# Attention scores of two batches with the keys in chunks of 128, 128, 128 and 64, where two pairs of heads share the chunk of 64

## The chip, the core and the metric

The kernel runs on one core of one Trainium2 chip. The metric is the device time of one execution in microseconds (us), lower is better. A core has engines that run at the same time, each through its own list of instructions in order: TensorE (PE, with its weight loads shown as PEld), VectorE (DVE), ScalarE (ACT), GpSimd (POOL) and SyncE (SP). Transfers between the main memory and the core's memory (SBUF) are issued from SP, ACT or POOL and run on 16 DMA engines. Products land in PSUM, a small memory that PE writes and that DVE and ACT read.

## What is computed

Attention with a softmax that has one added to its sum, and then a feed-forward layer with a squared ReLU:

```python
scores = scale * np.matmul(q, k.transpose(0, 1, 3, 2))
m = np.max(scores, axis=-1, keepdims=True)
e = np.exp(scores - m)
attn = e / (np.sum(e, axis=-1, keepdims=True) + np.exp(-m) + 1e-09)
x = np.matmul(attn, v)        # then laid out as 3584 tokens x 768
...
h = x @ w_in
r = np.maximum(h, 0.0)
out = (r * r) @ w_out
```

There are 8 batches, 12 heads, 448 positions and 64 numbers per head; w_in is 768 x 2048 and w_out 2048 x 768. All inputs are fp32; the kernel computes in fp16 with fp32 sums. It takes the exponentials without subtracting the maximum, so that the sum becomes sum(exp) + 1.

## The kernel before

**Layout.** Two heads make a pair (6 pairs in a batch): the queries and keys of a pair lie transposed in the tile `qk`, one head on rows 0 to 63 and the other on rows 64 to 127. A batch has 448 keys. They are taken in RUN = 4 chunks of P = 112; token 4p + s is row p of chunk s, since each partition loads four consecutive tokens. For a chunk, `scores` (L178) makes keys x queries in PSUM (tile `sp`, 112 rows, both heads side by side), one `exp` (L168) turns that into fp16 in the tile `et`, `add_chunks` (L209) adds the four chunks on DVE, `row_sums` (L239) sums over the 112 rows by a product with `ones` and makes the reciprocal of 1 + sum on ACT with a logarithm and an exponential (tile `rcp`), `values` (L232) makes the products of the four chunks with `vn` (tile `xp`), and `normalise` (L257) multiplies the two into `xt`, the input of the feed-forward layer.

**Units.** A unit is one pair and a range of its queries. Batch 0 is cut into queries 0 to 191 (units 0 to 5) and 192 to 447 (units 6 to 11), so that the feed-forward layer of its first 192 tokens can begin early. Batch 1 has units 12 to 17, batch 2 units 18 to 23, and so on. In the half units of batch 0 one exp takes two chunks (112 x 768 or 112 x 1024 numbers); in the others one exp takes one chunk of both heads (112 x 896).

**Start.** Batch 0's first three pairs are loaded as fp32 by SP (queries) and ACT (keys) into two buffers of the pool `e` (`load_natural`, L83), which has four buffers in all and also gives the `et` tiles: units 0 and 1 get the other two, and unit 2 gets the one that held the queries once they have been read. `cast` (L144) makes them fp16, 16 small transposes per pair on PE put both operands into one PSUM bank `tp` (`transposes`, L153), and DVE copies `tp` to `qk` (L164): for the first three pairs in two copies of half of the tokens, for the others in one. The other loads, all of `vn` among them (`load_v`, L77), are issued by POOL, which converts to fp16 on the way. Batches 1 and 2 are transposed in the same manner; from batch 3 on the transposes are done by DMA.

**Order.** The order of each engine's list is written out by hand. Loop L494 runs units 0 to 5, L523 units 6 to 11 and L561 units 12 to 17; in each, PE gets scores of the unit, transposes of a later pair, values and row sums of earlier units, and in between `drain` (L430) lets through so many steps of the first feed-forward product (`tile_in`, L297). At the end of unit 17 what is left of these is run (L590), then the row sums of unit 17 (L591). From L623 on, batches 2 to 7 go in groups of three units, with the second product (`tile_out`, L340) between the scores. Waits are set by the framework: an instruction waits for what it reads, and for the last readers of a buffer that it overwrites. PSUM has two buffers for `sp`, one for `xp` and three for `mp` (transposes, row sums, feed-forward).

In `et` of a half unit, chunk and head are addressed like this:

```python
return et[:, 0:RUN * 2 * n].rearrange("p (c h j n) -> p c h j n", c=2, h=2, j=2)[:, c, :, kk % 2, :]
```

The softmax here doesn't subtract the row's maximum and nothing guards it: scores larger than these inputs give would overflow.

## Time and profile before

The median of three runs is 412.54 us (412.3 to 412.69). The profiled execution took 412.49 us, of which 410.6 lie between its first and its last instruction (the span).

| | busy us | share of the span |
|---|---|---|
| PE | 401.0 | 98% |
| PEld | 259.0 | 63% |
| DVE | 289.8 | 71% |
| ACT | 234.4 | 57% |
| POOL | 36.3 | 9% |

"Busy" is the union of an engine's instructions; matmuls overlap and their ends are modelled, so a busy PE is not yet one at its peak. TensorE's clock was granted in full throughout (0.999). Some dates: the first exp starts at 6.78 us, unit 6's first at about 19 us, unit 12's first at 36.30 us, unit 17's row sums stand at 67.21 us, and the groups of three units begin right after. A group line gives the source line, engine, operation, output and inputs with their shapes, the count, then the total and the mean of one, and last the idle time of the engine ahead of it with what ended it.

### The profile page before, as it was taken

The page shows a single profiled execution, that of the slowest core. Times are in us where ns is not written, and L with a number is a line of the kernel's source. Part 1 is how long each engine was busy: PE and PEld are TensorE (multiplying, and loading weights), DVE is VectorE, ACT ScalarE, POOL GpSimd, SP SyncE. Part 2 cuts the span into 40 slices and gives each one's busy share as a digit, 9 for nine tenths or more (in the row PEclk, how much of TensorE's full clock was granted, in tenths as well). Part 3 has the DMA queues.
Part 4 walks back from the last instruction along what each step waited for, and adds up shares of the span by engine and source line. Part 5 has one row for each costly group of instructions (what it writes and reads, how often), then busy time and mean ns, then how long its engine had stood idle before and what let it go on. Part 6 is the DMA issues. An engine that isn't in the chain of part 4 may idle for free.

```text
span 410.6 us, 10685 instructions
## 1 busy us (share of the span) xinstructions
PE 401.0 (98%) x4715; PEld 259.0 (63%) x4715; DVE 289.8 (71%) x554; ACT 234.4 (57%) x312; POOL 36.3 (9%) x58
## 2 busy tenths in 40 slices
PE   7899998999999999999999999999999999999997
PEld 3577676755576666666566666667566665555664
DVE  3778896978976787777876788867876789186000
ACT  5998997667393745559383755739464663100111
POOL 7524030020000200001000030001000000000000
PEclk9999999999999999999999999999999999999999
DMA  9999999689114891499304992297102010010222
GB/s 203 197 198 197 203 202 219 127 132 219 60 42 107 135 219 25 98 183 182 100 2 114 168 179 64 77 188 124 41 2 69 11 41 2 38 40 0 78 77 78
DMA packets 75823, 45.58 MB, mean 111 GB/s; under 512 B 42560, under 2 KB 72000, under 8 KB 75456
## 3 DMA queue, kind: packets, MB, share of 16 engines
q0 software_dynamic: 28848, 22.16, 35.6%
q1 hardware_dynamic: 46208, 22.05, 23.1%
q8 instruction: 37, 0.61, 0.6%
q10 hardware_dynamic: 720, 0.69, 0.5%
q14 instruction: 10, 0.08, 0.1%
HBM read 45.69 MB, written 17.93 MB: 155 GB/s over the span
## 4 chain that ended last, share of the span: by engine, by line
PE 89%; ACT 4%; DVE 4%; DMA 1%; issue 1%
PE mp L286 24%; PE mp L352 17%; PE mp L288 11%; PE xp L286 8%; PE sp L201 6%; PE xp L352 5%; PE mp L236 5%; PE xp L288 3%; PE xp L236 3%; PE sp L189 3%; ACT et L169 3%; PE mp L250 2%; PE mp L158 1%; DMA et<-in_k_dram 1%; DVE qk L164 1%; ACT rcp L253 1%
## 5 line engine op out<-in xcount | busy, mean ns | idle before, releaser
L169 ACT ACTIVATE et<-sp 112x896 f16<-112x896 f32 (+2 forms) x144 | 125.2, 915 | 40.7 <-PE sp L201 30.6
L352 PE MATMUL mp<-wout,gs 64*128 64x384 f16 x896 | 115.2, 322 | 0.0
L286 PEld LDWEIGHTS <-win 128*64 128x64 f16 x1536 | 83.9, 110 | 45.6 <-issue 1.5
L286 PE MATMUL mp<-xt,win 128*64 128x448 f16 (+2 forms) x1200 | 107.0, 323 | 0.3 <-DVE qk L164 0.2
L293 DVE TENSOR_SCALAR rt<-mp 128x448 f16<-128x448 f32 (+2 forms) x96 | 59.7, 622 | 26.3 <-PE mp L286 13.8
L352 PEld LDWEIGHTS <-gs 64*128 64x128 f16 x1152 | 58.1, 94 | 21.1
L295 DVE TENSOR_TENSOR gs<-rt 128x448 f16<-128x448 f16 (+2 forms) x128 | 50.2, 392 | 4.4
L352 PE MATMUL xp<-wout,gs 64*128 64x384 f16 x256 | 53.1, 323 | 0.0
L253 ACT ACTIVATE rcp<-mp,one_b 128x448 f32<-128x448 f32 (+2 forms) x42 | 26.5, 630 | 41.9 <-PE mp L250 41.7
L361 ACT ACTIVATE ot<-mp 128x384 f32<-128x384 f32 (+1 forms) x16 | 7.6, 477 | 64.5 <-PE mp L288 48.2
L201 PE MATMUL sp<-qk 64*112 64x224 f16 x480 | 43.1, 258 | 0.0
L169 ACT ACTIVATE nn<-sp 112x896 f16<-112x896 f32 x48 | 41.7, 917 | 1.6
L201 PEld LDWEIGHTS <-qk 64*112 64x112 f16 x480 | 30.6, 128 | 14.2 <-issue 3.6
L286 PE MATMUL xp<-xt,win 128*64 128x448 f16 x336 | 36.5, 352 | 0.0
L288 PEld LDWEIGHTS <-gs 128*128 128x128 f16 x256 | 24.4, 98 | 15.1 <-issue 0.4
L236 PEld LDWEIGHTS <-vn 112*64 112x64 f16 x432 | 22.4, 109 | 15.4 <-issue 3.9
L288 PE MATMUL mp<-wout,gs 128*128 128x384 f16 (+1 forms) x192 | 30.3, 317 | 0.0
L214 DVE TENSOR_TENSOR es<-et 112x896 f16<-112x896 f16 x30 | 18.7, 623 | 15.8 <-ACT et L169 15.3
L254 ACT ACTIVATE rcp<-rcp 128x448 f32<-128x448 f32 (+2 forms) x48 | 27.7, 577 | 1.5
L189 PE MATMUL sp<-qk 64*112 64x448 f16 (+2 forms) x192 | 25.8, 320 | 1.4 <-ACT et L169 0.6
L216 DVE TENSOR_TENSOR es<-es,half 112x896 f16<-112x896 f16 x42 | 26.2, 623 | 1.0
L293 DVE TENSOR_SCALAR rt<-xp 128x448 f16<-128x448 f32 x32 | 19.9, 622 | 8.2 <-PE xp L286 6.7
(63 smaller groups left out, 340.0 us busy)
## 6 DMA issues: line engine op xcount, KB each, us to landing
vn<-in_v_dram POOLq DMA_DIRECT2D x7, 672.0 KB, 9.0
out_dram<-ot SPq DMA_DIRECT2D x9, 384.0 KB, 2.3
win<-in_moe_w_in_dram POOLq DMA_DIRECT2D x8, 384.0 KB, 14.2
wout<-in_moe_w_out_dram POOLq DMA_DIRECT2D x4, 768.0 KB, 18.0
stage_q<-in_q_dram POOLq DMA_DIRECT2D x4, 676.0 KB, 11.3
stage_k<-in_k_dram POOLq DMA_DIRECT2D x4, 676.0 KB, 14.7
out_dram<-ot SPq DMA_DIRECT2D x8, 288.0 KB, 9.0
out_dram<-ot SPq DMA_DIRECT2D x9, 192.0 KB, 2.7
```

The lines of the kernel that those rows point to most:

```text
L169: nc.scalar.activation(out=out_, in_=in_, func=AF.Exp, scale=scale)
L189: nc.tensor.matmul(sp[:, h, o:o + n], qk[r, 1, x + P * kk:x + P * kk + P], qk[r, 0, x + q0:x + q0 + n], start=True, stop=True)
L201: nc.tensor.matmul(sp[:, odd, h * (S // 2):(h + 1) * (S // 2)], qk[r, which, kx:kx + 2 * P - 1:2], qk[r, 0, x:x + S // 2], start=True, sto ...
L216: nc.vector.tensor_add(es, es, half[:, 0:2 * S])
L236: nc.tensor.matmul(xp[64 * h:64 * h + 64, o:o + n], vns[b][:, 2 * pr + h, kk, :], of_head(chunk(et, u, kk // 2, kk), u, h), start=(kk == 0 ...
L253: nc.scalar.activation(out=rcp[:, 0:m], in_=zp[:, 0:m], func=AF.Ln, bias=one_b)
L254: nc.scalar.activation(out=rcp[:, 0:m], in_=rcp[:, 0:m], func=AF.Exp, scale=-1.0)
L286: nc.tensor.matmul(out_[x:x + 64], lhsT[:, x:x + 64], rhs, start=start, stop=stop)
L288: nc.tensor.matmul(out_, lhsT, rhs, start=start, stop=stop)
L293: nc.vector.tensor_scalar(out=rt[:, 0:m], in0=hp[:, 0:m], scalar1=0.0, scalar2=None, op0=ALU.max)
L295: nc.vector.tensor_mul(gs[:, f0:f0 + per, t0 % RING:t0 % RING + n], r, r)
L352: nc.tensor.matmul(o[:, 0:w], g[x:x + 64], wout[x:x + 64, fb, n0:n0 + w], start=(fb == 0), stop=(fb == NFFB - 1))
```

## The change

Batches 0 and 1 (`WIDE`) take their keys in three chunks of 128 and one of 64. Key 3p + kk, for keys 0 to 383, is row p of chunk kk; keys 384 to 447 are the last chunk. Two neighbouring pairs share one tile for the last chunk: pair j of the two on rows 64j to 64j + 63, so that one exp serves both. One unit of the two "owns" it: the odd one among units 0 to 5, the even one among units 6 to 17. The owner's `et` is kept until the other unit's values are done.

- **Exps.** The unit that isn't the owner has 3 chunks instead of 4: in batch 1 three exps instead of four, in batch 0 a second exp of half size. All have 128 rows instead of 112.
- **Scores.** The last chunk is four products of 64 x 64 tiles (two heads, two pairs) instead of two of 64 x 112.
- **Sums.** DVE adds only the three chunks of 128 (two additions, from four chunks in three, or in batch 0 two, of which one was double size). `row_sums` has a second product per head, of the shared chunk with `halves`, a matrix that is 1/256 on the unit's own 64 rows and zero on the others.
- **Values.** The last product of a head has 128 rows of `vn`, of which the other pair's 64 are zero; DVE clears them at the start, for both batches (`clear_v`).
- **Loads.** `vn` of these batches comes in 128 partitions of 3 tokens, and the last 64 tokens in four loads more (`load_last_v`): for batch 0 as fp32 from SP and ACT, into the unused end of the two buffers that hold the raw queries and keys, whence DVE converts them in unit 1 (`cast_last_v`); for batch 1 from POOL.
- **Copies to `qk`.** The keys are put into the order of the tokens while they are copied, which reads `tp` with a step of 112 numbers; the queries keep their order. So a pair of these batches has two copies instead of one, the first three pairs of batch 0 three instead of two (keys; queries 0 to 191; queries 192 to 447). Pair 0's first copy of queries is made by ACT.
- **Buffers.** From unit 18 on every third `et` lies in one of the two `nn` buffers, in turn, where it was two in six before, beginning with unit 22. Batches 2 to 7 compute as before.

```diff
     def load_v(b, p0, p1):
...
+        if b in WIDE:
+            nc.gpsimd.dma_start(out=vns[b][:, hs, 0:RW], in_=v[b, hs, 0:SW].rearrange("h (p t) d -> p h t d", t=RW))
...
+    def load_last_v(b):
+        for j in range(2):
+            for h in range(2):
+                to, src = last_v(b, j, h)
+                if b:
+                    nc.gpsimd.dma_start(out=to, in_=src)
+                else:
+                    (nc.sync, nc.scalar)[j].dma_start(out=raw_v(j, h), in_=src)
...
+    def cast_last_v():
+        for j in range(2):
+            for h in range(2):
+                nc.vector.tensor_copy(last_v(0, j, h)[0], raw_v(j, h))
+
+    def clear_v(b):
...
+        for j in range(2):
+            nc.vector.memset(rows[64 - 64 * j:128 - 64 * j, j, :, :, RW, :], 0.0)
...
-        parts = (0, S // 2, S) if b == 0 and pr < 3 else (0, S)
-        for x, y in zip(parts, parts[1:]):
-            nc.vector.tensor_copy(qks[b][:, 0:2, pr * S + x:pr * S + y], tp[:, :, x:y])
+        o = qks[b][:, :, pr * S:(pr + 1) * S]
+        if b not in WIDE:
+            nc.vector.tensor_copy(o[:, 0:2], tp[:, :, 0:S])
+            return
+
+        nc.vector.tensor_copy(o[:, 1].rearrange("p (n s) -> p n s", s=RUN), tp[:, 1, 0:S].rearrange("p (s n) -> p n s", s=RUN))
+        if b == 0 and pr < 3:
+            if pr == 0:
+                nc.scalar.activation(out=o[:, 0, 0:FIRST], in_=tp[:, 0, 0:FIRST], func=AF.Copy)
+            else:
+                nc.vector.tensor_copy(o[:, 0, 0:FIRST], tp[:, 0, 0:FIRST])
+            nc.vector.tensor_copy(o[:, 0, FIRST:S], tp[:, 0, FIRST:S])
+        else:
+            nc.vector.tensor_copy(o[:, 0], tp[:, 0, 0:S])
...
+    def wide_scores(u, et, c, last):
+        b, pr, q0, n = u
+        qk = qks[b]
+        kks = (0, 1) if c == 0 else (2, 3) if last else (2,)
+        two = [] if n == S else s_psum.tile([128, 2, 512], FP32, name="sp")
+        for kk in kks:
+            sp = s_psum.tile([128, 2, 512], FP32, name="sp") if n == S else two
+            o = 0 if n == S else kk % 2 * n
+            pairs = (pr,) if kk < RW else (pr // 2 * 2, pr // 2 * 2 + 1)
+            for h in range(2):
+                r = slice(64 * h, 64 * h + 64)
+                for j, of in enumerate(pairs):
+                    x = of * S
+                    keys = slice(x + kk, x + SW, RW) if kk < RW else slice(x + SW, x + S)
+                    to = slice(0, 128) if kk < RW else slice(64 * j, 64 * j + 64)
+                    nc.tensor.matmul(sp[to, h, o:o + n], qk[r, 1, keys], qk[r, 0, x + q0:x + q0 + n],
+                                     start=True, stop=True)
...
+            if u[0] in WIDE:
+                nc.vector.tensor_add(es, (e[:, 0], es)[step], e[:, 1 + step])
...
+            nc.vector.tensor_add(s, (e[:, 0, :, 0], s)[step], (e[:, 0, :, 1], e[:, 1, :, 0])[step])
...
+            parts = [(ones, total), (halves[:, u[1] % 2], last_chunk(i))] if u[0] in WIDE else [(ones[0:P], total[0:P])]
...
+        if i >= 3 * NPAIR and i % 3 == 2:
+            ets[i] = nat.tile([128, RUN * 2 * S], FP16, name=f"nn{i // 3 % 2}")
...
+    def owns(i):
+
+        return i % 2 == (i < NPAIR) and units[i][0] in WIDE
...
         if i:
             sums(i - 1)
+        if i == 1:
+            cast_last_v()
         if i > 1:
-            scores(u, et, 1)
+            visit(i, 1)
```

## The prediction, made before the change was run

> **What bounds the kernel now.** I read the page's first part, then busy time by stretch, then the chain of work that ended last, and the groups by form for prices.

> ```profile
> PE 401.0 (98%) x4715; PEld 259.0 (63%) x4715; DVE 289.8 (71%) x554; ACT 234.4 (57%) x312; POOL 36.3 (9%) x58
> ```

> PE bounds the whole, but the change lies in the first 69 us (batches 0 and 1). Busy time there, by stretch (start:end, length, busy us and count per engine, clock, DMA share, GB/s):

> ```profile
> 6.00:10.40 4.40, 3.88 (x61) 2.12 (x61) 3.23 (x10) 3.62 (x6) 2.64 (x4) 1.00 1.40 212
> 10.40:18.30 7.90, 7.39 (x123) 4.62 (x122) 6.14 (x14) 7.44 (x12) 4.55 (x6) 1.00 1.46 197
> 18.30:36.30 18.00, 16.33 (x296) 12.34 (x295) 14.10 (x29) 15.76 (x20) 5.46 (x7) 1.00 1.45 197
> ...
> 42.60:67.20 24.60, 23.05 (x356) 16.72 (x355) 22.04 (x42) 20.69 (x28) 3.51 (x5) 1.00 1.38 207
> ```

> The columns after the length are PE, PEld, DVE, ACT, POOL. Units 2 to 5 (second line) are ACT's: 7.44 of 7.90 us. In units 6 to 11 (third) ACT and PE are both nearly full; from unit 13 on (last line) PE has 1.55 us idle in 24.6 and DVE 2.6. The chain says the same step by step:

> ```profile
> 9.52 0.69 DVE qk L164 x2
> ...
> 21.43 1.54 ACT et L169 x2
> ...
> 36.30 3.35 ACT et L169 x4
> ...
> 47.24 0.53 PE sp L189 x4
> 47.76 0.31 PE mp L250 x2
> 48.08 0.76 PE xp L236 x8
> ...
> 66.53 0.64 DVE es L216
> 67.21 0.40 PE mp L250 x2
> ```

> The reader is to see three things: DVE's copies to `qk` carry the start; ACT's exps carry the middle; PE carries batch 1, until one wait of 1.13 us at its end, where PE stands for unit 17's sums. Products of 64-row halves run two at a time (eight of 448 in 0.76 us, 0.19 per two), and a group of another tile shape costs about 0.15 us more (four score products 0.53 instead of 0.38). After 69 us PE is full in every stretch that I looked at, up to 110 us, so a shift of that point goes through to the end.

> Prices, from the groups by form:

> ```profile
> L169 ACT ACTIVATE et<-sp 112x1024 f16<-112x1024 f32 x12 | 11.8, 1016 | 1.0 <-PE sp L189 0.7
> L169 ACT ACTIVATE et<-sp 112x768 f16<-112x768 f32 x12 | 9.4, 806 | 1.0 <-PE sp L189 0.9
> L164 DVE COPY qk<-mp 128x896 f16<-128x896 f16 x14 | 8.4, 618 | 1.0 <-PE mp L158 1.0
> L164 DVE COPY qk<-mp 128x448 f16<-128x448 f16 x6 | 2.1, 386 | 2.2 <-PE mp L158 2.2
> ```

> [...] The new copy of the keys reads with a step of 112[...] contiguous fp16 from PSUM 386 ns for 448 numbers, fp32 from PSUM (L293, 128x448) 622; no row shows a stepped fp16 read. [...] four 64x64 tiles at once are not in the trace.

> **The change, part by part.**

> *Exps (ACT, removed).* Batch 1: three exps of 0.917, 2.75 us. Batch 0: from the two rows above a number costs 0.82 ns, so half sizes take 0.49 and 0.60: three times 0.32 and three times 0.42, 2.2 us. Pair 0's copy of 192 queries adds about 0.33 (L361 takes 277 ns for 128, 383 for 256). 128 rows cost what 112 do, since 896 numbers per row stay 896.

> *DVE.* Sums: batch 1 loses one addition of 0.623 per unit, 3.7 us; batch 0 swaps 0.551 + 0.358 for 2 x 0.358 and 0.689 + 0.422 for 2 x 0.422, 6 x 0.19 + 6 x 0.27 = 2.8. Copies to `qk`: 0.62 (keys, stepped) + 0.386 for 0.618, +0.39 in nine pairs; the first three go from 0.77 to 0.91 (pair 0) and 0.62 + 0.25 + 0.29 = 1.16 (the two rows give 154 ns + 0.518 per number). In all +4.4. If the stepped read cost nothing extra, 0.386, it would be +1.6; I take 0.62. Four casts of 64x192: the one near row is 0.43 for 512 (L150), a memset of 64 takes 0.11; I take 0.25 each, 1.0 in sum, ends 0.5 and 1.7. Zeroing `vn` and `halves`, about 1.3 us, lies in the 3.24 us in which DVE waits for the first queries: nothing, unless POOL's first `vn` load (1.49 us) has to wait for the zeros. That is at most 0.6 for the rest of POOL's queue, the fourth pair's loads among it, which land just ahead of their transposes at 10.27. DVE's total hardly moves; its place does.

> *PE.* Row sums: two products more per unit, 0.19 (448), 0.11 (256), 0.08 (192). Last chunk: per two units two score pairs become one set of four tiles, less one pair's time, but with one more change of shape, 0.15. Net per two units: 2 x 0.19 − 0.19 + 0.15 = 0.34, three times = 1.0 in batch 1; 0.26 and 0.23 in batch 0's halves, three times each = 1.5. If four tiles don't overlap, 0.19 more per two units (+0.6 in batch 1); if the change of shape is hidden, 0.45 less.

> *Start, units 0 to 5 (to 18.25 us, unit 5's second exp).* The keys' copy starts at 5.92 as before. Keys 0.62, ACT's copy 0.33 after it: unit 0's scores at 6.95 (6.36 before). DVE is then 0.6 late for the next cast, and pair 1's scores need 0.62 + 0.25 where one copy of 0.386 was enough: 9.1 (8.13). Pair 2 in the same way: copies done at 11.6. Now a **new wait**: unit 2's exps write the buffer that held the raw queries, and that is free only after `cast_last_v`, which stands on DVE behind those copies and unit 0's sums (0.66 with overlap): three casts later it is 12.9, against 10.38 in the trace: +2.5[...]. Behind the waiting exp on ACT stand all other exps; PE waits with them, since `sp` has two buffers. From there ACT has two half exps less (−0.64), but DVE, with the keys' copies of pairs 3 to 5 (+1.17, less four sums at 0.19), is now last at the row sums: +0.4. I take **+2.0** at unit 5's end; ends +1.0 and +2.9.

> *Units 6 to 11.* ACT loses 1.26, but PE has only about 1.0 us idle between 20.3 and 36.3 and gains 0.7 of work; unit 5's sums are 0.2 shorter. The gain is cut off by PE: **−0.3**, ends −0.9 and +0.4.

> *Units 12 to 17.* Unit 13 has its exp less where PE now waits 0.41 for ACT (42.56): −0.4. At the end one addition instead of two stands behind the last `drain`: −0.6 of the 1.13. PE's work +1.0. Other ACT savings are slack: ACT has 3.9 us idle there. **0.0**, ends −0.9 and +0.8.

> *Loads.* SP and ACT issue two more each (0.46 us a piece), ahead of ACT's table load; ACT idles 1.28 us after it: nothing. They land behind the third pair's, which took 6.0 us at most from issue; the casts come at 12.2: nothing. POOL's four more for batch 1 go behind a load issued at 25.48 that lands 16.4 us later, at 41.9; first use is 43.10. Rows of 256 bytes instead of 1024; 0.1 MB at the 197 GB/s of the stretch is 0.5 us, at a quarter of that 2. PE, itself two us later, then has 1 us in hand: nothing, at worst +0.5. POOL idles 7.7 us before 34.14, which hides the issues; the later `wout` lands near 60 and is read at 67.75, which hides 1 to 2 us of DMA time. The `nn` buffer that unit 20 now takes was last read at 61.3: nothing.

> *Sum.* +2.0 − 0.3 + 0.0 = **+1.7 us**. It is made on the profiled execution (412.49 us, span 410.6), which agrees with the three runs (412.3 to 412.69): 412.54 + 1.7 = 414.2. With all lower ends −0.8, with all upper ones +4.1 (4.6 with the late load). A shift of 0.2%, 0.8 us, is about what a measurement of this kernel can tell from none.

> **Rivals.**

> 1. *The start's delay is swallowed, and the run is faster: 411.2.* For it: PE idles some 4.4 us between 10 and 67 us, DVE and ACT lose 6.5 and 4.9 us, and ACT is what the chain names most before 42 us. If the stepped copy costs 0.39[...], the wait for the casts shrinks to about +1.2 and the three later copies of keys to +0.5; ACT's half exps (0.64) and DVE's sums (3 x 0.19) leave +0.5 of the start, and the lower ends of the two later stretches, 0.9 each, make it −1.3. It decides once unit 5's second exp is less than 1 us late. Against it: DVE stands in the chain at 9.52, with the copies that grow.
> 2. *A wash, 412.8.* The start costs +2.0 as forecast, but the delayed units 6 to 11 lie in ACT's stretch and take 1.3 back, and batch 1's end 0.5. For it: 15.76 of 18.0 us ACT in that stretch. Against: PE is 16.33 there.
> 3. *Late data, 416.5.* POOL's queue is held by the zeros (+0.6), batch 1's last keys' values come after PE needs them (+0.5), four tiles do not overlap (+1.2). Against: the DMA slack shown above.

> **Chances.** The likeliest, 414.2: 0.50. Rival 1: 0.22, rival 2: 0.20, rival 3: 0.08. Faster 0.22, same 0.20, slower 0.58. The range from 411.0 to 416.4 takes in the forecast's own ends to the larger part (411.7 to 416.6) and half of rival 1; some 0.1 is left out below and 0.05 above. The forecast alone would be 413.0 to 416.4.

> **What would show it.** In the profile after: the keys' copy at 0.62 us; unit 2's first exp at 12 to 13 us, and ACT's idle time in front of it put down to DVE; row sums of four products per unit in some 0.5 us; ACT emptier by 2 to 3 us from 42 us on without any gain; PE waiting some 0.5 us instead of 1.13 for unit 17's sums; that point at 68.5 to 69.5 instead of 67.21. I am wrong if unit 2's exps start before 11.5, if the keys' copy takes 0.39, or if PE's busy share in units 6 to 11 falls.

## The result, and the profile after

The changed kernel takes **419.88 us** (median of four runs, 419.77 to 420.36) against 412.5: ratio 1.0181, interval 1.0164 to 1.0199. It is slower by 7.4 us. The sign was forecast, the size was not: 414.2 had been said, at most 416.4.

The first part of the page shows nothing of this. PE has 36 instructions more and 4.9 us more of busy time in a span that is 7.4 us longer (418.0 against 410.6); DVE and ACT are about as busy as forecast (ACT 3.9 us less than before, where 4.6 had been said):

```profile
PE 405.9 (97%) x4751; PEld 260.2 (62%) x4751; DVE 289.4 (69%) x570; ACT 230.5 (55%) x310; POOL 39.3 (9%) x62
...
PEclk8599999999999999999999999999999999999999
```

The second line is the clock granted to PE in 40 slices of the span. Its second slice, 10.4 to 20.9 us, is a 5: the granted clock was at half there. Before, the clock was full throughout. Busy time by stretch of the changed kernel (columns as in the prediction: PE, PEld, DVE, ACT, POOL, clock, DMA share, GB/s):

```profile
6.00:8.00 2.00, 0.71 (x9) 0.33 (x9) 0.28 (x1) 1.23 (x2) 1.66 (x3) 0.93 1.36 228
8.00:10.00 2.00, 1.40 (x21) 0.97 (x22) 0.97 (x3) 1.55 (x3) 0.35 (x1) 0.50 1.43 192
10.00:20.00 10.00, 8.72 (x106) 5.12 (x102) 6.83 (x20) 5.31 (x10) 5.54 (x7) 0.50 1.47 196
```

and of the kernel before:

```profile
6.00:8.00 2.00, 1.77 (x26) 0.89 (x25) 1.32 (x5) 1.80 (x3) 1.56 (x2) 1.00 1.35 234
...
10.00:20.00 10.00, 8.73 (x145) 5.67 (x146) 7.99 (x18) 9.16 (x14) 5.65 (x8) 1.00 1.45 197
```

From 10 to 20 us PE is as busy as before (8.72 us; before 8.73), but does 106 products in that time where it did 145 (not all of the same shapes). The busy share doesn't tell the two apart; the count and the clock (0.50 against 1.00) do. Just ahead of it, from 6 to 8 us, PE had next to nothing to do: 0.71 us, against 1.77 before.

ACT's timeline of the changed kernel says why (start, length, engine, line, operation; idle time before it in brackets, with what ended it; ACTq are its DMA issues):

```profile
0.75 1.46 ACTq L128 DMA_DIRECT2D et<-in_k_dram  x3
2.25 3.04 ACTq L101 DMA_DIRECT2D et<-in_v_dram  x2
5.31 1.28 ACT L460 ACT_TABLE_LOAD   x1 [5.31 <-DMA et<-in_k_dram]
6.61 0.63 ACT L184 ACTIVATE flatk<-et 112x512 f16<-112x512 f32 x1
...
15.86 1.19 ACT L216 ACTIVATE et<-sp 128x768 f16<-128x768 f32 x2 [2.53 <-PE sp L240]
...
25.19 1.71 ACT L216 ACTIVATE et<-sp 128x768 f16<-128x768 f32 x2
```

and in the kernel before:

```profile
2.24 1.28 ACT L379 ACT_TABLE_LOAD   x1 [2.24 <-issue]
4.80 0.63 ACT L148 ACTIVATE flatk<-et 112x512 f16<-112x512 f32 x1 [1.28 <-DMA et<-in_k_dram]
```

Three loads of keys are issued in 1.46 us, but the two added loads of values take 3.04, and the table load behind them starts at 5.31 instead of 2.24 us. What ended the wait is the landing of a load of keys. So the first cast of keys starts at 6.61 us (before 4.80), and PE's transposes wait 2.09 us for it.

Four dates place the loss:

| start of | before | after | later by |
|---|---|---|---|
| unit 2's first exp | 10.38 | 15.86 | 5.5 |
| unit 5's second exp | 18.25 | 25.19 | 6.9 |
| unit 12's first exp | 36.30 | 43.39 | 7.1 |
| unit 17's row sums | 67.21 | 74.19 | 7.0 |

Nearly all of it is in units 0 to 5. From there to unit 17's sums the two kernels take the same time, 48.96 and 49.00 us, and the 0.4 that is left lies behind them.

### The profile page after: what moved, and what is told of

It reads as the page before. It is cut to its first block, busy times and chain, and to the rows that moved or that the text cites. A ratio compares the mean times of both kernels' runs of the same rounds, so it can differ in the third digit from the quotient of the medians.

```text
span 418.0 us, 10790 instructions
## 1 busy us (share of the span) xinstructions
PE 405.9 (97%) x4751; PEld 260.2 (62%) x4751; DVE 289.4 (69%) x570; ACT 230.5 (55%) x310; POOL 39.3 (9%) x62
## 4 chain that ended last, share of the span: by engine, by line
PE 86%; DMA 9%; DVE 2%; POOL 1%; ACT 1%; issue 0%; POOLq 0%; DVEq 0%
PE mp L359 23%; PE mp L425 17%; PE mp L361 10%; PE xp L359 8%; PE sp L269 6%; PE xp L425 5%; PE mp L305 5%; DMA vn<-in_v_dram 5%; DMA win<-in_moe_w_in_dram 4%; PE xp L361 3%; PE xp L305 3%; PE mp L323 2%; PE sp L257 1%; PE sp L240 1%; POOL nn L135 1%; ACT et L216 1%
## 5 line engine op out<-in xcount | busy, mean ns | idle before, releaser
L216 ACT ACTIVATE et<-sp 112x896 f16<-112x896 f32 (+5 forms) x141 | 121.0, 900 | 50.0 <-PE sp L269 30.6
L216 ACT ACTIVATE nn<-sp 112x896 f16<-112x896 f32 x48 | 42.2, 917 | 1.0
L361 PEld LDWEIGHTS <-gs 128*128 128x128 f16 x256 | 24.4, 98 | 15.1 <-issue 0.4
L305 PEld LDWEIGHTS <-vn 112*64 112x64 f16 (+1 forms) x432 | 22.6, 111 | 15.5 <-issue 3.8
L361 PE MATMUL mp<-wout,gs 128*128 128x384 f16 (+1 forms) x192 | 30.3, 317 | 0.0
L281 DVE TENSOR_TENSOR es<-et 112x896 f16<-112x896 f16 x24 | 14.9, 622 | 15.5 <-ACT et L216 15.5
L283 DVE TENSOR_TENSOR es<-es,half 112x896 f16<-112x896 f16 x36 | 22.4, 623 | 0.8
L432 DVE TENSOR_SCALAR ot<-mp 128x384 f32<-128x384 f32 x28 | 15.6, 557 | 9.6 <-PE mp L425 6.1
```

Source lines behind the costliest of these rows:

```text
L216: nc.scalar.activation(out=out_, in_=in_, func=AF.Exp, scale=scale)
L283: nc.vector.tensor_add(es[0:P], es[0:P], half[0:P])
L305: nc.tensor.matmul(xp[64 * h:64 * h + 64, o:o + n], vns[b][r, 2 * pr + h, kk, :], of_head(e, u, h), start=(kk == 0), stop=(kk == RUN - 1))
L361: nc.tensor.matmul(out_, lhsT, rhs, start=start, stop=stop)
L432: nc.vector.tensor_scalar(out=ot[:, n0:n0 + w], in0=op[:, 0:w], scalar1=OUT_SCALE, scalar2=None, op0=ALU.mult)
```

## The experiments

Each median stands against runs of the kernel before on the same chip, 412.5 to 412.7.

**The added loads.** First all four loads of the last values on SP, so that ACT issues none:

```diff
-                    (nc.sync, nc.scalar)[j].dma_start(out=raw_v(j, h), in_=src)
+                    nc.sync.dma_start(out=raw_v(j, h), in_=src)
```

> The changed kernel with all four loads of batch 0's last 64 tokens of v issued by SP, none by ACT. Theory A (ACT's fifth load holds back its table load, PE idles 2 us and its clock falls to half until 21 us): the first cast of keys starts near 4.8 us instead of 6.61, the clock stays full, 414 to 416 us. Rival B (the delay is DVE's copies and the wait for the buffer of the raw queries, as predicted): 418.5 us or more.

Measured: 418.48 us (ratio 1.014, 1.0125 to 1.0156), 1.4 less and short of what I expected. The table load is back at 2.25 us and the cast of keys at 4.89, yet the clock falls all the same. Stretches of this kernel:

```profile
6.00:8.00 2.00, 0.76 (x9) 0.35 (x10) 1.50 (x3) 1.34 (x3) 1.65 (x3) 1.00 1.34 230
8.00:10.00 2.00, 1.65 (x23) 0.82 (x23) 1.31 (x5) 0.62 (x2) 0.01 (x1) 0.57 1.42 184
10.00:20.00 10.00, 9.06 (x108) 5.27 (x106) 6.74 (x20) 5.60 (x9) 5.65 (x7) 0.50 1.47 195
```

PE is again nearly empty from 6 to 8 us, now for another reason: it waits 0.76 us for pair 0's copies by DVE and then ACT (0.17 before), and 0.48 for DVE's next cast. Those are the delays that the prediction had counted, but not what they do to the clock.

Then the other way round, the four loads alone in the kernel before, into a tile that nothing reads; and after that the same bytes in two loads, one on SP and one on ACT:

```diff
+    raw_last = consts.tile([128, 2, NPAIR // 2 * D], FP32)
+    for j in range(2):
+        for h in range(2):
...
+            (nc.sync, nc.scalar)[j].dma_start(out=to, in_=src)
```

> The kernel before with nothing but the four loads added, two on SP and two on ACT, into a tile that nobody reads. Theory A: the table load starts near 5.3 us instead of 2.24, the clock falls, 415.5 to 419 us. Rival B: the loads are hidden as predicted, 412.2 to 413.

> The kernel before with the same bytes as in the run with four loads added, but as one load on SP and one on ACT, eight in all on the two queues instead of ten. If what held the table load was the ninth and tenth load's wait for the first ones to land: the table load starts near 3 us, 412.3 to 413. If it was the issue time of small rows or the traffic: 414 or more (415.8 with four).

Measured: 415.77 us with four loads (1.0089, 1.0057 to 1.0121), 413.39 with two (1.0035, 1.0017 to 1.0052). ACT's timeline of the first:

```profile
2.24 3.05 ACTq L384 DMA_DIRECT2D raw_last<-in_v_dram  x2
5.32 1.28 ACT L385 ACT_TABLE_LOAD   x1 [5.32 <-DMA et<-in_k_dram]
```

and of the second:

```profile
2.24 0.70 ACTq L383 DMA_DIRECT2D raw_last<-in_v_dram  x1
2.97 1.28 ACT L384 ACT_TABLE_LOAD   x1 [2.97 <-issue]
```

One load more per queue costs ACT 0.70 us of issue; with two more, ten in all on SP and ACT, ACT stands until a load of keys has landed, and the two take 3.05 us. SP stands in the same way in the changed kernel: its two added loads take 2.75 us, and 1.4 of them are a wait for the landing of a load of queries. The two loads cost 0.8 us (the table load is 0.7 later, and PE's transposes of pair 3 wait for data, 0.2 us each for their queries and keys), which lies between the two forecasts; the landing wait and what follows from it is 2.4 more. In the profiled run with four loads the clock also fell, from 8 us to about 11 (0.50 in the stretch from 8 to 10), but another of its runs kept the full clock and took 415.77 us too, so those 2.4 don't need the clock.

**The clock.** Eight idle products (PE's, of a result that nothing reads) more in the changed kernel between pair 0's two sets of transposes, the place of the 2.09 us wait:

```diff
+            if (b, pr, i) == (0, 0, 1):
+                keep_warm(8)
```

> The changed kernel with eight idle products more on PE between pair 0's transposes of queries and of keys, where PE waits for ACT. The late table load stays. Theory A with the clock as the larger part: the clock stays full, the cast of keys still starts at 6.6 us, 416 to 417.5 us. If the lost clock is hidden behind DVE and ACT (rival B): 419.5 or more. If the late table load is all: the same 419.5 or more.

Measured: 420.01 us (1.018). By the forecast this speaks for the rivals, but the clock had not stayed full: it holds until 11.4 us and then is at half until 21.7. PE has 1.10 us of work from 8 to 10 us and 1.33 from 10 to 12. So next, with all loads on SP, idle products in the gaps of units 0 to 3 (20 more by the edit, 35 instead of 15 in the trace; the expectations below call them 16); and the same with the loads divided as in the changed kernel, with the eight of the run above:

```diff
-    keep_warm(1)
+    keep_warm(5)
...
+        if i == 0:
+            keep_warm(2)
...
-            keep_warm(1)
+            keep_warm(5)
...
+        if i == 2:
+            keep_warm(4)
...
-            keep_warm(1 + i // 5)
+            keep_warm({1: 5, 3: 3, 5: 2}[i])
```

> The four loads on SP, and 16 idle products more on PE in units 0 to 3, put where PE waits for DVE or ACT. Theory A2 (what costs most is TensorE's clock, which falls to half because PE now waits too much in units 0 to 2, with or without the late table load): the clock stays above 0.95, unit 5's second exp starts by 21 us (about 24.3 in the run with the loads on SP alone), 414 to 416 us. Rival B (DVE's order sets the pace and the clock only fills gaps): the clock is full and the time falls by 0.7 us at most, 417.8 or more.

> The changed kernel (loads on SP and ACT as in it, late table load kept) with the same idle products and eight more between pair 0's transposes. Theory A2: the clock stays full; what is left of the late table load is its own delay, 1.2 to 2.0 us more than the run with the loads on SP and the idle products, 415.5 to 417.5. If the late table load is what brings the clock down: the clock falls again and it stays near 419.5.

Measured: 416.51 us (1.0095) and 418.33 (1.0144), both at full clock and each above the range that its theory gave. The difference, 1.8 us, is the late table load at full clock (the eight lie in the wait that it makes). But the chain of the first shows idle products on the path:

```profile
5.73 1.18 PE mp L533 x5
6.92 0.36 PE sp L240 x6
...
8.33 1.19 PE mp L533 x5
9.51 0.57 PE sp L240 x10
```

Line 533 is the idle product; the scores of line 240 start when it ends. So I measured their own price, the same 20 in the kernel before, and cut them to 12 (27 in the trace; "9" in the expectations) in the version with the loads on SP:

> The kernel before with the 16 idle products more, at the same places: what they cost by themselves where the clock is full anyway. If they only fill waits: 412.3 to 412.9 us. If they lie on the path, as the chain of the run with 16 suggests: 413.2 to 415.

> The four loads on SP and 9 instead of 16 idle products more on PE, none of them where the chain of waits showed them on the path. If the idle products themselves cost something in the run with 16 and 9 still keep the clock full: 415.6 to 416.2 us (416.5 with 16). If 9 are too few, the clock falls: 417.5 or more. If they cost nothing: 416.4 to 416.6.

Measured: 415.51 us with 20 in the kernel before, +2.9 and above its forecast, where they have nothing to repair; 416.04 us (1.0081, 1.0066 to 1.0096) with 12 in the changed kernel, still at full clock. So holding the clock gained 418.48 − 416.04 = 2.4 us with the loads on SP, and what the 12 cost in place is still in the 416.04. With the late table load it gained 419.88 − 418.33 = 1.55, with 28 idle products.

When does the clock fall, and when does it come back? Half clock lasted 13.66 us in the changed kernel. In the other four traces in which it fell, the mean clock of stretches of 2 us gives 13.64 us with the loads on SP and with a buffer of its own (below), 10.24 with the eight idle products and 3.40 in the kernel before with four loads: within 0.04 us, four, three and one times 3.41. The changed kernel, cut into pieces of that length at the points where its clock changed:

```profile
4.30:7.71 3.41, 1.32 (x20) 0.58 (x18) 0.43 (x1) 1.91 (x2) 3.36 (x5) 1.00 1.23 270
7.71:11.13 3.42, 2.61 (x24) 1.24 (x23) 1.96 (x6) 2.04 (x4) 1.34 (x2) 0.50 1.43 193
11.13:14.54 3.41, 2.93 (x34) 1.50 (x36) 2.22 (x9) 1.51 (x2) 2.90 (x4) 0.50 1.51 193
14.54:17.95 3.41, 2.82 (x36) 1.78 (x38) 3.10 (x9) 1.50 (x3) 1.53 (x2) 0.50 1.47 202
17.95:21.37 3.42, 3.42 (x41) 1.98 (x38) 2.01 (x5) 2.42 (x4) 0.94 (x2) 0.50 1.45 194
21.37:24.78 3.41, 3.27 (x56) 1.99 (x54) 2.17 (x6) 2.53 (x5) 1.55 (x2) 1.00 1.45 196
```

The clock falls behind a piece with 1.32 us of PE's work and returns behind the first one that PE fills (3.42); the three at half clock ahead of that one had 2.61, 2.93 and 2.82. With the loads on SP, PE's timeline, cut in the same way, has 2.03 us ahead of the fall, 2.69 to 3.19 in the three pieces at half clock without a return and 3.41 in the one ahead of the return. For the other three there are stretches of 2 us: the two that take in the 3.41 us ahead of the fall hold 1.51 us of PE's work in 4 us (a buffer of its own), 1.94 (the kernel before with four loads) and 2.43 (eight idle products), the two up to just behind the return 3.95 to 4.00. The kernel before kept the full clock, and between 4 and 408 us no 3.41 us of it, wherever they are cut, have less than 2.28 us of PE's work. The fall comes at another date in each version, at 7.71 us here, at 8.28 with the loads on SP, at 9.60 with a buffer of its own, so that a gap can fall into one piece or be divided between two; whether that decides was not tested.

Nor does every run of a kernel lose or keep its clock alike. Of the 20 runs with two loads 16 took 412.98 to 413.54 us at full clock, and four took 415.91 to 417.77 at a mean clock of 0.983 to 0.988; one of 25 runs of the kernel before took 416.99 at 0.988. These runs are 2.5 to 4.4 us longer, but they have no trace, and whatever else delayed them may be part of that. Against a price that is the same everywhere stands one run of the version below with a buffer of its own and the late table load: it took 419.51 us at 0.999, only 0.3 to 1.0 less than the other three at 0.982 to 0.984. So 2.4 us is the price in one pair of versions and not a general one.

**The buffer wait.** The prediction's "new wait" of unit 2's exps, taken away by giving the raw values a tile of their own, in the changed kernel and in the version with 20 idle products:

```diff
+    raw_last = consts.tile([128, 2, NPAIR // 2 * D], FP32)
...
-        x = NPAIR // 2 * 512
-        return whole["qk"[h]][64 * j:64 * j + 64, x:x + NPAIR // 2 * D].rearrange("p (r d) -> p r d", d=D)
+        return raw_last[64 * j:64 * j + 64, h].rearrange("p (r d) -> p r d", d=D)
```

> The changed kernel with the raw last tokens of v in a buffer of their own, so that unit 2's exps need not wait for the casts. Rival B: unit 2's first exp starts over 1 us earlier (before 14.8 us instead of 15.86) and 1.0 to 2.0 us of the time go, 418 to 418.9. Theory A: DVE and the slow PE take over the wait, at most 0.5 us less, 419.4 to 419.9.

> The same as the run with loads on SP and more idle products, and the raw last tokens of v in a buffer of their own. If the wait of unit 2's exps for the casts is real and was only hidden by the slow clock: 0.7 to 1.5 us less than that run. If DVE's work behind it sets the pace: within 0.4 of it.

Measured: 419.90 and 416.67 us; nothing is gained. The wait exists, as ACT's timeline of the version with 12 idle products names it:

```profile
12.90 1.19 ACT L216 ACTIVATE et<-sp 128x768 f16<-128x768 f32 x2 [2.09 <-DVE vn L110]
```

Without it unit 2's exps start earlier (12.65 instead of 13.33 us with 20 idle products), and unit 3's later (15.51 instead of 14.96). DVE, with the same casts, copies and sums on its list, sets the pace behind them: in both versions the chain of waits runs through these casts and copies.

**DVE's work at the start.** Without the four casts (the last 64 rows of batch 0's values are zero then), and with the keys copied without a step (scores and values then belong to different keys), each in the version with 20 idle products:

```diff
-        nc.vector.tensor_copy(o[:, 1].rearrange("p (n s) -> p n s", s=RUN), tp[:, 1, 0:S].rearrange("p (s n) -> p n s", s=RUN))
+        nc.vector.tensor_copy(o[:, 1], tp[:, 1, 0:S])
```

> The run with the loads on SP and the idle products, without the four casts of the last tokens of v: for batch 0 these rows of v stay zero, so its last 64 keys add to the sums and not to the values. At full clock, if DVE sets the pace of units 0 to 5: the casts' 1.24 us go, 415.0 to 415.6 us (416.5 with them). If they lie beside other work: 416.1 or more.

> The same run with the casts, but the keys copied without the step of 112, so that they lie in the order of the transposes: scores and values then belong to different keys. If the stepped read (0.62 instead of 0.39 us, nine times in the first 21 us and in batch 1) sets the pace: 0.6 to 1.2 us less, 415.3 to 415.9. If not: 416.2 or more.

Measured: 416.04 us (−0.5, between the two forecasts) and 415.50 (−1.0, as forecast for a step that sets the pace). Then the last values of batch 0 by POOL, which converts them on the way, so that the casts and SP's loads go and the values are complete; with 20 and with 12 idle products, and the latter also without the step:

```diff
-                if b:
-                    nc.gpsimd.dma_start(out=to, in_=src)
-                else:
-                    (nc.sync, nc.scalar)[j].dma_start(out=raw_v(j, h), in_=src)
+                nc.gpsimd.dma_start(out=to, in_=src)
...
-    load_last_v(0)
...
     load_natural(0, 3, 4)
+    load_last_v(0)
...
-        if i == 1:
-            cast_last_v()
```

> The changed kernel with batch 0's last tokens of v loaded by POOL, converted on the way and placed behind pair 3's loads, so with no casts and no load more on SP or ACT, and with the idle products. If the casts are what can be saved: 415.0 to 415.8, still slower than before. If the small loads hold up POOL's queue and the weights behind it: 416.5 or more.

> Batch 0's last tokens of v by POOL, no casts, and the 9 idle products: the whole change with its new waits at the start repaired. If the idle products cost 0.5: 414.7 to 415.2 us. In any case slower than the kernel before if the copies to qk and the added products of the row sums are what is left; 412.9 or less if not.

> The same with the keys copied without the step, so that scores and values belong to different keys. If the stepped read is still on the path once the casts are gone: 0.6 to 1.2 us less, 413.7 to 414.5. If casts and copies hide each other: within 0.3 of the run before it.

Measured: 415.47, 414.69 (1.0053, 1.0038 to 1.0068) and 413.84 us (1.0027, 1.0017 to 1.0038). With loads, casts and clock repaired the change costs 2.1 us, the 12 idle products included, and 0.85 of that is the step.

**Batch 1 alone.** `WIDE = (1,)`, batch 0 computed as in the kernel before:

> Batch 0 as in the kernel before, batch 1 alone with chunks of 128 and 64. The prediction's step for units 12 to 17 (PE's added row sums against one wait less each at the start and the end): 0.0 with ends -0.9 and +0.8, 411.6 to 413.4, while ACT loses three exps. If the gain of ACT came through: 410.5 or less. If the four small tiles and row sums cost more than thought: 413.5 or more.

Measured: 412.97 us over 20 runs (1.0011, 1.0004 to 1.0018). Stretch 43 to 68 us of the kernel before:

```profile
43.00:68.00 25.00, 23.45 (x362) 16.95 (x362) 22.40 (x42) 20.66 (x29) 3.51 (x5) 1.00 1.38 211
```

and of batch 1 alone:

```profile
43.00:68.00 25.00, 23.46 (x368) 16.39 (x370) 19.89 (x40) 18.87 (x26) 4.71 (x7) 1.00 1.39 211
```

DVE does 2.5 and ACT 1.8 us less there, and PE is as full as before: work was taken from two engines that had slack. From unit 12's first exp to unit 17's sums it takes 30.76 us instead of 30.91, but that exp itself starts 0.87 later. Of this 0.48 stands already at unit 5's second exp (18.73 instead of 18.25 us) and was not traced; the rest comes in units 6 to 11, where PE now waits 0.50 us for a copy of batch 1's pairs to `qk`.

No version that was tried beats the kernel before.

## Why the prediction was wrong

The loss, split along a row of versions that differ by one part each:

| from, to | us | what |
|---|---|---|
| changed kernel, all loads on SP | 1.4 | late table load (1.8 at full clock) |
| to 12 idle products | 2.4 | half clock, less what these products cost |
| to POOL's loads, no casts | 1.35 | the casts and SP's loads |
| to keys without the step | 0.85 | the stepped copy |
| to the kernel before | 1.2 | the rest, the 12 idle products included |

**The step that failed** is "*Loads.* SP and ACT issue two more each (0.46 us a piece), ahead of ACT's table load; ACT idles 1.28 us after it: nothing". A price of issue was taken from loads that never had to wait. In the changed kernel each queue does wait within its two added loads, for the landing of a load of keys or queries, and the engine stands with it: the two took 3.04 us on ACT and 2.75 on SP, and not 0.92. The table load, and the cast of keys behind it, were not set against that. A second failure runs through the whole sum: every term was priced at full clock. Nothing in the prediction asked whether PE, emptied at 6 to 8 us, would keep it. In the changed kernel it didn't, and with the table load in time the counted delays alone (0.76 and 0.48 us of PE's waiting) were enough to bring it down. These two, late table load and half clock, are 3 to 4 of the 7.4 us; of the rest the forecast had 1.7, and the term of the start was too small.

The other steps:

- *Start, +2.0 (ends 1.0 and 2.9).* At full clock and with the table load in time, unit 5's second exp stands at 20.89 us (12 idle products), **+2.6**. The mechanism was right in its parts: the keys' copy took the forecast 0.62 us (no more than an estimate, since no row of the kernel before showed a stepped read), ACT's copy came after it (0.33) and not beside it, and unit 2's exps started at 12.90 (forecast 12.9), released by the casts; that the two agree so closely is partly luck, since it is 13.33 with 20 idle products. Mis-sized were the casts, 0.34 each instead of 0.25, 0.4 in sum; the other 0.2 were not traced (idle products lie there too):

```profile
L203 DVE COPY qk<-mp 128x448 f16<-128x448 f16 x12 | 7.4, 620 | 7.2 <-PE mp L194 7.2
...
L110 DVE CAST vn<-et 64x192 f16<-64x192 f32 x4 | 1.2, 342 | 0.0
L206 ACT ACTIVATE qk<-mp 128x192 f16<-128x192 f16 x1 | 0.3, 331 | 1.1 <-DVE qk L203 1.1
L216 ACT ACTIVATE et<-sp 128x384 f16<-128x384 f32 x3 | 1.5, 487 | 0.0
L216 ACT ACTIVATE et<-sp 128x512 f16<-128x512 f32 x3 | 1.8, 595 | 0.1
```

  (Groups by form of the changed kernel: total and mean in us and ns, then idle time before.) One reading was wrong: the buffer wait was taken for what carries the +2.0, but without it nothing is won. It stands beside DVE's list, which is as long.
- *Units 6 to 11, −0.3.* They took 18.20 us instead of 18.05 (+0.15), inside the ends: ACT's saving is cut off by PE, which ends ACT's waits there (1.45 us ahead of unit 12's first exp, before 0.63).
- *Units 12 to 17, 0.0.* They took 30.80 instead of 30.91 us (−0.1), and batch 1 alone −0.15. The wait at the end was 0.47 instead of 1.13, as forecast:

```profile
74.19 0.38 PE L323 MATMUL mp<-es,ones 128*64 128x448 f16 x2 [0.47 <-DVE es L279]
```

- *Late data.* POOL's first load of `vn` started at 1.47 us (before 1.49), so the zeros held nothing, and the end of batch 1 was not late. Four tiles at once: four products of 64 x 448 in tiles of 64 x 64 took 0.38 us together, where two in tiles of 64 x 128 took 0.37, so they do overlap. The changed kernel's trace puts one wait of PE, 0.50 us at 42.36, down to a load of `vn`, and the chain on its page runs through POOL's loads up to there (DMA 9%). The version with 12 idle products has the same wait of 0.50 at the same product, ended by DVE's copy to `qk`, as has batch 1 alone; so I take it that the load only landed at that moment. That rival found no support, and rivals 1 and 2 fell with the start.

**What stays open.** What half clock cost in the changed kernel as it stands is not fixed better than by the 1.55 us above and the one run that speaks for less. How a load of PE between 2.03 and 2.28 us in a piece of 3.41, or between 3.19 and 3.41 at half clock, would be taken these traces do not show. The last 1.2 us were not split further: part of it is the 12 idle products, the second and third copies to `qk`, the added products of the row sums, and the 0.4 of batch 1 alone.

## What to carry to other kernels

Before an extra load is put on a queue at the start, count the loads of SP and ACT that are under way together: here eight went through (0.70 us for ACT's fourth), and with ten both engines stood until a load of keys or queries had landed (3.04 and 2.75 us for two loads each), with everything behind them on the lists. Price a delay near the start of a PE-bound kernel twice, once as time and once by what it leaves of PE's load over the next few microseconds, since here the clock halved behind 3.41 us with 1.32 or 2.03 us of work; then look at the granted clock and the count of products, never at the busy share alone. A version that loses its clock in one run of five, as the one with two loads did (four of 20), is to be run often: a median of four can hide it. And taking work from engines that have slack bought nothing here, while the copies and casts that made it possible stood where the chain ran.
